# Splitting the buffers of the forms in two, and loading x for the first half's residual into the part of forms 0 and 1

## The chip, the cores and the metric

The kernel runs on one core of a Trainium2 chip. The metric is the device time of one execution in microseconds (us), inputs and outputs in HBM. A run's time is taken without the profiler; one further execution was recorded by the hardware profiler, and everything that is said below of what waits for what comes from that trace.

## The reference

A block with a linear attention and a gated feed-forward network on the same normalized input, S = 2048 tokens of D = 512 features, F = 1792, 32 heads of 16. All numbers are float32.

```
xn = layernorm(x)
q, k, v = split(xn @ wqkv)                      # 32 heads of 16
pq, pk = phi(q), phi(k)                         # phi(t) = (t + 1 if t > 0 else exp(t)) + 1e-6
kv, z = sum_s pk^T v, sum_s pk                  # per head
s = ((pq @ kv) / (pq @ z + 1e-6)) @ wo
g = silu((gelu(xn @ w_gate) * (xn @ w_up)) @ w_down)
out = x + s * g
```

## The kernel before

**Products.** float32 matmuls are done as three passes of split numbers (a high part h and a low part l: hh, then hl and lh; `sum3`, L498). Each block product is a Strassen-like scheme of seven products: for two operands cut into 2 x 2 blocks, seven combinations of blocks ("forms", numbered 0 to 6 by slot) are made of either side, and product i (1 to 7) multiplies weight form a with data form b, `PRODUCTS` (L32): 1 takes data form 0, 2 takes 1, 3 takes 2, 4 takes 6, 5 takes 3, 6 takes 4, 7 takes 5. In PSUM four running results are kept, X (products 1, 6, 7, 4, one added on the other), Y (2), Z (5, 3) and V.

**Stages.** (1) Norm, transposes, the products with wqkv, and sums for kv and z; the forms of xn are left in two large tiles of SBUF, `XT["h"]` and `XT["l"]` (L544, pool "xf", 7 slots x 4 groups of 256 tokens in transposed form). There is room for one half of the tokens, so the forms of the first four groups are written to HBM (`spill_x`, L770, in 8 DMAs of 896 KB) and come back later. (2) The FFN over the second half of the tokens (p = 1), then (3) over the first (p = 0). (4) The last stage: s = pn @ M, where M holds kv and wo together, multiplied by g and added to x.

**The last stage** works on half p = 1, then p = 0, and within each on two column blocks c = 0, 1: four blocks (1,0), (1,1), (0,0), (0,1), with the numbers 0 to 3 in the names of the PSUM tiles and the saved results (SX2 is X of block (0,0), su2_3 the second saved X of block (0,1)). In `s_forms` (L1325) the forms of pn are made: for p = 1 in the rows of `XT["h"]` and `XT["l"]`, which the FFN has done with (row r = 7a + s for form s of operand half a, L1315), for p = 0 in tiles sf0h to sf1l of pool "wp". `s_quad` (L1348) issues the products of a block and, on VectorE and GpSimd, the sums, the product with g and the residual: `x = o + r` (L1380), o being the tile "xp" with x. The results X are copied out of PSUM by ScalarE (`esaved`, L1050) into a ring of three buffers ("fe"): a copy waits until the third copy before it has been read, and TensorE may add its next product to X only after the copy.

**x for the residual** comes with `x_again` (L1408). For p = 1 it takes four tiles of pool "dp"; for p = 0 one tile "xp0" that lies in the place of `XT["h"]`, loaded by four DMAs of 512 KB:

```
whole = tile_in("xf", "h", [P, KT, HALF], F32, "xp0", 0)
```

A tile in another's place waits until every reader of the earlier tile is done.

**What sets the order.** `Plan` holds all operations with costs and dependences, TensorE's order is written out by hand (`pe_keys`; at the end L1433 to L1443), and a list scheduler with late times finds the order on the other engines, improved by a list of random changes (`STEPS`, L91, `order`, L345). VectorE, ScalarE, GpSimd and TensorE then work in exactly that order. The DMAs are all issued by SyncE, in one queue and in order; their place there follows from the program as it is emitted, and each waits in that queue for what it needs. The last blocks' products run in the order 6, 5, 7 of a block, 1 and 2 of the next, then 3 and 4.

Of the kernel before, what the change touches and what calls it, by code (L numbers as in the profile page):

```python
# [11 lines left out]
F32 = mybir.dt.float32  # L12
F32R = mybir.dt.float32r
# [4 lines left out]
P = 128  # L18
# [55 lines left out]


class Op:
    __slots__ = ("eng", "cost", "fn", "pre", "suc", "key", "name", "port", "kb", "n", "out", "use", "way", "land")


class Plan:  # L80
# [8 lines left out]
    ROUNDS = 14  # L89
    MARGIN = (0.2, 0.2, 3.0)  # L90
    STEPS = (12, 17, 30, 37, 54, 58, 64, 68, 88, 91, 95, 112, 120, 130, 135, 178, 219, 243, 254, 272, 291, 296, 307, 334, 350, 358, 391, 399, 421, 482, 518, 595, 713, 745, 884, 952, 1037, 1318, 1332, 1383, 1390, 1412, 1459, 1532, 1540, 1563, 1676, 1910, 1984, 2062, 2080, 2109, 2148, 2154, 2161, 2184, 2185, 2285, 2316, 2343, 2539, 2627, 2682, 2732, 2736, 2755, 2779, 2791, 2797, 2850, 2885, 3006, 3525, 3544, 3782, 3810, 3819, 4355, 4555, 4804, 4809, 5047, 5174, 5351)  # L91
    WAIT = 0.3
    FIXED = 4

    def __init__(self):
        self.ops = []
        self.first = 0

    def do(self, eng, cost, fn, out, *ins, more=(), key=None, name="", kb=0, kind="load"):

        op = Op()
        views = [v for v in (out, *ins) if isinstance(v, View)]
        if eng == "ACT" and any(v.psum for v in views):
            cost -= 0.04
        op.eng, op.cost, op.key, op.name = eng, cost, key, name
        op.fn = lambda: fn(out(), *[i() if isinstance(i, View) else i for i in ins])
        op.pre, op.suc = set(), []
        op.way, op.land, gap = self.MOVES[kind]
        op.kb = kb / self.RATE + gap if kb else 0.0
        op.port = eng == "POOL" or eng == "DVE" and cost > 0.25 and not any(v.psum for v in views)  # L110
        outs = set(out.res)
        for m in more:
            outs.update(m.res)
        op.out = outs
        op.use = {r for i in ins if isinstance(i, View) for r in i.res} | outs
        for i in ins:
            if isinstance(i, View):
                for r in i.res:
                    if r not in outs:
                        op.pre.update(r.writers)  # L120
                        if i.psum:
                            for d in r.readers:
                                if d.eng != eng:
                                    a, b = (op, d) if eng == "ACT" else (d, op)
                                    b.pre.add(a)
                                    a.suc.append(b)
                        r.readers.append(op)
        for r in outs:
            op.pre.update(r.writers)
            op.pre.update(r.readers)  # L130
            r.writers, r.readers = [op], []
        for v in (out, *more, *ins):
            if isinstance(v, View) and v.gen:
                assert not v.gen.over, name
                if v.gen.prev:
# [206 lines left out]
        width, size, share = rng.choice((4.0, 10.0, 25.0)), rng.choice((0.2, 0.6, 2.0)), rng.choice((0.1, 0.4, 1.0))  # L342
        return [v + rng.uniform(-size, size) if t - width < a < t + 2.0 and rng.random() < share else v for v, a in zip(late, at)]

    def order(self, pe_keys):  # L345

        late, done = self.first_order(pe_keys)
        at = self.plan_times(done)
        for seed in self.STEPS:
            late = self.nudged(late, at, seed)  # L350
            _, done = self.run(self.wide, late)
            at = self.plan_times(done)
        self.at = {self.ops[i]: t for i, t in enumerate(at)}
        self.log(max(at))
        return [self.ops[i] for i in done]
# [22 lines left out]
def kernel(  # L378
# [13 lines left out]
    nc = tc.nc  # L392
# [3 lines left out]
    KT = D // P  # L396
    NT = S // P
    NC = 512
# [4 lines left out]
    plan = Plan()  # L403
    do = plan.do
    pe_keys = []
# [51 lines left out]
    def ext(ap):  # L457
        return View((), lambda: ap)

    def dma(dst, src, kb, kind="load"):  # L460
        do("SP", 0.475, lambda o, i: nc.sync.dma_start(o, i), dst, src, kb=kb, kind=kind, name=kind)
# [76 lines left out]

    XR = {(hl, s, j): Res() for hl in "hl" for s in range(7) for j in range(4)}
    XT = {}  # L540

    def x_tiles(gen, names="hl"):
        for hl in names:
            XT[hl] = tile_in("xf", hl, [P, 7, 4, 2, P], F32R, f"X{hl}{gen}", 0)  # L544

    x_tiles(0)

    def xblock(hl, lo, hi, j):

        return XT[hl].part([XR[hl, s, j] for s in range(lo, hi)], (slice(None), slice(lo, hi), j)).map(  # L550
            lambda ap: ap.rearrange("p s k c -> p s (k c)"))

    def xslot(hl, s, j):
        return XT[hl].part([XR[hl, s, j]], (slice(None), s, j))

    def xall(hl, s):
        return XT[hl].part([XR[hl, s, j] for j in range(4)], (slice(None), s))

    def by_slot(v):
        return v.map(lambda ap: ap.rearrange("p (s k) c -> p s (k c)", k=2))  # L560
# [202 lines left out]
    def gacc(t):  # L763
        if not gps:
            gps.extend(bank(4 + c, f"gps{c}") for c in range(KT))
        for c in range(KT):
            cs = (slice(None), slice(c * P, (c + 1) * P))
            sum3(("G", t, c), gps[c], [([v[cs] for v in xn_s[t]], pk_s[t])], t == first_g, t == last_g, "gacc")

    def spill_x(n):  # L770
        for hl in "hl":
            dma(x_d[hl](n, (slice(None), slice(None), n)), xblock(hl, 0, 7, n).map(lambda ap: ap.bitcast(F32)), 896, "pieces")

    def first_products(n):
        ta = tokens[n][0]
# [533 lines left out]
    ms = [weights("W", a, f"ms{a}") for a in range(2)]  # L1309
    for a in range(2):  # L1310
        load_weights(("m", a), ms[a])
    xforms = {}
    for a in range(2):
        for s in range(7):
            r = 7 * a + s  # L1315
            for hl in "hl":
                xforms[hl, a, s] = View([XR[hl, r // 2, 2 * (r % 2) + n] for n in range(2)], XT[hl].map(
                    lambda ap, r=r: ap.rearrange("p s j k c -> p (s j k c)")[:, r * NC:(r + 1) * NC]).get, XT[hl].gen)
    BR = [12, 13, 14, 6, 7, 8, 9, 10, 11]
    HALF = 2 * NC  # L1320
    LAST = (1, 0)
# [86 lines left out]
    def x_again(p):  # L1408

        got = {}  # L1410
        if not p:
            whole = tile_in("xf", "h", [P, KT, HALF], F32, "xp0", 0)
        for k in (0, 2, 1, 3):
            got[k] = tile_in("dp", ring("br", BR), [P, HALF], F32, f"xp{p}{k}", 4) if p else whole.part(
                [Res() for _ in range(4)], (slice(None), k))
            dma(got[k], ext(xt[k * P:(k + 1) * P, p * HALF:(p + 1) * HALF]), 512, "first")
        return got

    forms, gg, xps = {}, {}, {}
    for p in (1, 0):  # L1420
        forms[p] = s_forms(p)
        if p:
# [67 lines left out]
```

## Time and profile before

| what | us |
|---|---|
| median of 3 runs | 605.6 (604.96 to 605.67) |
| profiled execution, its own time | 605.75 |
| its span, first to last instruction | 604.0 |
| TensorE busy | 593.9 |
| VectorE busy | 471.4 |
| GpSimd busy | 357.1 |
| ScalarE busy | 334.8 |
| mean granted TensorE clock | 0.993 |

The engines' names in the profile are PE (TensorE), PEld (its weight loads), DVE (VectorE), ACT (ScalarE), POOL (GpSimd) and SP or SPq (SyncE, which issues the DMAs). A row of a timeline has the start, the length, the engine, the line and the operation with its tiles, out<-in, and in brackets how long the engine had been idle and who released it. Names of tiles have their numbers left out there: SX is SX0 to SX3, Xh and Xl are the tiles of forms. One DMA of the profile is the issue; its data lands some microseconds later. In the table by stretches the columns are the stretch and its length, the busy time of each engine with its count of instructions, the granted clock (PEclk), the busy share of DMA and its GB/s. "DMA to landing" gives the least, median and longest time from issue to landing for the DMAs of one tile.

### The profile page before, as it was taken

How to read it: one execution, taken by the hardware profiler on the slowest of the kernel's cores; microseconds unless marked ns; L12 is line 12 of the kernel's file. 1: busy time of each engine (PE TensorE's matmuls, PEld its weight loads, DVE VectorE, ACT ScalarE, POOL GpSimd, SP SyncE). 2: the span in 40 equal slices, each digit the busy share in tenths (PEclk: the TensorE clock that was granted, in tenths of full speed). 3: DMA queues.
4: the chain of work that ended last, by engine and by line, in shares of the span. 5: the costliest groups of instructions: out<-in, count | busy, mean ns of one | idle time of the engine just before them, and what ended most of it. 6: DMA issues, size and time to landing. Idle time of an engine off the chain costs nothing.

```text
span 604.0 us, 8229 instructions
## 1 busy us (share of the span) xinstructions
PE 593.9 (98%) x2696; PEld 490.7 (81%) x2696; DVE 471.4 (78%) x698; ACT 334.8 (55%) x611; POOL 357.1 (59%) x300
## 2 busy tenths in 40 slices
PE   8999999999999999999999999999999999999994
PEld 7888888888888888888888888887888888887883
DVE  6999988785788878898888947556656776889995
ACT  6777777876676654564464146455134640477730
POOL 4844654525778865977598226437226752667664
PEclk9999999999999999999999999999999999999997
DMA  7459522258759637864769986888499996998347
GB/s 244 141 180 306 192 70 89 89 171 281 278 194 328 244 123 262 331 226 148 260 216 398 337 314 209 301 293 281 153 288 320 318 328 199 363 329 292 108 136 281
DMA packets 59370, 145.24 MB, mean 240 GB/s; under 512 B 5568, under 2 KB 17088, under 8 KB 59328
## 3 DMA queue, kind: packets, MB, share of 16 engines
q1 hardware_dynamic: 59328, 144.73, 68.8%
q8 instruction: 21, 0.34, 0.2%
q14 instruction: 21, 0.17, 0.1%
HBM read 82.05 MB, written 62.65 MB: 240 GB/s over the span
## 4 chain that ended last, share of the span: by engine, by line
PE 95%; DMA 2%; DVE 1%; ACT 0%; SPq 0%; issue 0%; DVEq 0%; ACTq 0%
PE FX L508 25%; PE FZ L508 13%; PE DX L508 13%; PE gps L508 7%; PE DZ L508 6%; PE FY L508 6%; PE X L508 5%; PE DY L508 3%; PE SX L508 3%; PE Z L508 3%; PE q L508 2%; PE k L508 2%; DMA xp<-in_xt 1%; PE Y L508 1%; PE ptq L1165 1%; PE pt L677 1%
## 5 line engine op out<-in xcount | busy, mean ns | idle before, releaser
L508 PE MATMUL FX<-Xh,w 128*128 128x512 f32 x448 | 152.4, 390 | 0.0
L1073 POOL TENSOR_TENSOR h<-h,g 128x512 f32<-128x512 f32 x42 | 63.1, 1508 | 69.9 <-DVE h L492 65.2
L508 PEld LDWEIGHTS FX<-Xh,w 128*128 128x128 f32 x448 | 83.7, 188 | 17.1
L492 POOL TENSOR_TENSOR h<-h,h 128x512 f32<-128x512 f32 x56 | 83.7, 1494 | 17.8 <-DVE hf5l L492 4.4
L508 PE MATMUL FX<-Xl,w 128*128 128x512 f32 x224 | 87.3, 390 | 0.0
L508 PE MATMUL FZ<-Xh,w 128*128 128x512 f32 x224 | 78.0, 390 | 0.0
L486 ACT COPY fu<-FX 128x512 f32<-128x512 f32 x56 | 32.9, 587 | 60.5 <-PE FX L508 46.4
L508 PE MATMUL gps<-pks,xns 128*128 128x512 f32 x192 | 51.2, 391 | 0.0
L508 PEld LDWEIGHTS FX<-Xl,w 128*128 128x128 f32 x224 | 42.1, 188 | 8.7
L508 PEld LDWEIGHTS FZ<-Xh,w 128*128 128x128 f32 x224 | 42.0, 188 | 8.6
L753 POOL TENSOR_TENSOR zacc<-zacc,kp 128x512 f32<-128x512 f32 x16 | 24.8, 1551 | 34.6 <-DVE kp L742 34.4
L508 PE MATMUL FZ<-Xl,w 128*128 128x512 f32 x112 | 43.7, 390 | 0.0
L492 POOL TENSOR_TENSOR u<-q,zacc 128x512 f32<-128x512 f32 x16 | 22.2, 1407 | 34.6 <-ACT g L1065 15.5
L508 PEld LDWEIGHTS gps<-pks,xns 128*128 128x128 f32 x192 | 35.9, 188 | 7.4
L1099 DVE TENSOR_TENSOR acc<-acc,DX 128x512 f32<-128x512 f32 x48 | 32.5, 684 | 9.2 <-PE DX L508 8.8
L508 PE MATMUL FY<-Xh,w 128*128 128x512 f32 x112 | 39.0, 389 | 0.0
L492 DVE TENSOR_TENSOR h<-fu,FZ 128x512 f32<-128x512 f32 x28 | 19.1, 684 | 22.7 <-PE FZ L508 15.4
L486 ACT COPY fe<-FX 128x512 f32<-128x512 f32 x28 | 16.5, 588 | 34.5 <-PE FX L508 31.1
L492 DVE TENSOR_TENSOR g<-fu,FZ 128x512 f32<-128x512 f32 x28 | 19.1, 682 | 20.3 <-PE FZ L508 13.3
L1065 ACT ACTIVATE g<-g 128x512 f32<-128x512 f32 x42 | 26.6, 633 | 13.4 <-DVE g L492 13.4
L508 PE MATMUL X<-kq,Xh 128*128 128x512 f32 x96 | 30.8, 397 | 0.0
L1099 DVE TENSOR_TENSOR acc<-acc,DZ 128x512 f32<-128x512 f32 x32 | 21.8, 682 | 10.5 <-PE DZ L508 8.9
(423 smaller groups left out, 1599.0 us busy)
## 6 DMA issues: line engine op xcount, KB each, us to landing
w_d<-w SPq DMA_DIRECT2D x36, 512.0 KB, 4.8
w<-w_d SPq DMA_DIRECT2D x36, 512.0 KB, 5.1
wd_d<-wd SPq DMA_DIRECT2D x21, 512.0 KB, 4.8
wd<-wd_d SPq DMA_DIRECT2D x21, 512.0 KB, 5.4
x<-in_first SPq DMA_DIRECT2D x16, 256.0 KB, 3.9
q_d<-qp SPq DMA_DIRECT2D x16, 256.0 KB, 2.0
q<-q_d SPq DMA_DIRECT2D x16, 256.0 KB, 5.1
pn_d<-pT SPq DMA_DIRECT2D x8, 512.0 KB, 6.1
```

The source lines that it names most:

```text
L486: do("ACT", act(n), lambda o, i: nc.scalar.copy(o, i), dst, src, name=name)
L492: do(eng, c, lambda o, p, q: getattr(e, f"tensor_{op}")(o, p, q), dst, a, b, name=name)
L508: nc.tensor.matmul(o, v[i], v[i + 1], start=start and part == 0 and i == 0, stop=stop and part == 1 and i == len(v) - 2, skip_group_check=on)
L677: nc.tensor.transpose(o[:, k, :], a[:, k * P:(k + 1) * P], b)
L753: do("POOL", pool(D), lambda o, i: nc.gpsimd.tensor_add(o, o, i), zacc, p0, name="zacc")
L1065: curved("gelu", do("ACT", curve(NC), lambda o, i: nc.scalar.activation(o, i, AF.Gelu_apprx_tanh), g, ps if e is None else g, name="gelu"))
L1073: do("POOL", pool(NC), lambda o, i: nc.gpsimd.tensor_mul(o, o, i), h, g, name="h")
L1099: do("DVE", dve(NC), lambda o, i: nc.vector.tensor_add(o, o, i), a, ps, name="acc")
L1165: nc.tensor.transpose(v[:, k, :], u[:, k * P:(k + 1) * P], idn)
```

## The change

`XT["h"]` and `XT["l"]` become two tiles each: one with slots 0 and 1 (forms 0 and 1 of xn), one with slots 2 to 6; the places in SBUF together are as large as before. In the last stage the forms of the half p = 1 are laid out so that forms 0 and 1 of both operand halves fill the first tile (`REST` has the rows of the others). `x_again(0)` takes two tiles, in the place of the first tile of h (for k = 0, 1) and of l (for k = 2, 3), so its loads wait for the products 1 and 2 of the blocks (1,0) and (1,1), and not for all products of that half. The spills, which now come from two tiles, are two DMAs each, 256 and 640 KB, 16 in all.

The planner is given the old dependences while it makes its first order and its list of changes (`held`, `steady`, `hold_rows`), then the true ones; `MORE`, a list for further changes, is empty.

```diff
@@ class Plan
+    MORE = ()
...
+    def steady(self, pe_keys):
+
+        for op, pre in self.held:
+            op.kept = set(op.pre)
+            self.free_of(op, pre)
+        late, done = self.first_order(pe_keys)
+        late, done, at = self.improved(late, done, self.plan_times(done), self.STEPS)
+        for op, _ in self.held:
+            self.free_of(op, op.kept)
...
+        _, done = self.run(self.wide, late)
+        return late, done, self.plan_times(done)
@@ the tiles of the forms
+    XCUT = ((0, 2), (2, 7))
 
     def x_tiles(gen, names="hl"):
         for hl in names:
-            XT[hl] = tile_in("xf", hl, [P, 7, 4, 2, P], F32R, f"X{hl}{gen}", 0)
+            for i, (lo, hi) in enumerate(XCUT):
+                XT[hl, i] = tile_in("xf", f"{hl}{i}", [P, hi - lo, 4, 2, P], F32R, f"X{hl}{i}{gen}", 0)
@@ the spills
+    def move_both(o, a, b):
+        nc.sync.dma_start(o[:, 0:2], a)
+        nc.sync.dma_start(o[:, 2:7], b)
+
     def spill_x(n):
         for hl in "hl":
-            dma(x_d[hl](n, (slice(None), slice(None), n)), xblock(hl, 0, 7, n).map(lambda ap: ap.bitcast(F32)), 896, "pieces")
+            a, b = [xblock(hl, *XCUT[i], n).map(lambda ap: ap.bitcast(F32)) for i in range(2)]
+            do("SP", 0.475, move_both, x_d[hl](n, (slice(None), slice(None), n)), a, b, kb=896, kind="pieces", name="pieces")
@@ the rows of the forms of the half p = 1
+    REST = (8, 9, 6, 7, 10, 11, 12, 13, 4, 5)
...
-            r = 7 * a + s
+            r = 2 * a + s if s < 2 else REST[5 * a + s - 2]
@@ x_again
-        if not p:
-            whole = tile_in("xf", "h", [P, KT, HALF], F32, "xp0", 0)
+        before = XT["h", 0].gen.ops | XT["h", 1].gen.ops
+        whole = {} if p else {hl: tile_in("xf", f"{hl}0", [P, 2, HALF], F32, f"xp0{hl}", 2) for hl in "hl"}
         for k in (0, 2, 1, 3):
-            got[k] = tile_in("dp", ring("br", BR), [P, HALF], F32, f"xp{p}{k}", 4) if p else whole.part(
-                [Res() for _ in range(4)], (slice(None), k))
+            got[k] = tile_in("dp", ring("br", BR), [P, HALF], F32, f"xp{p}{k}", 4) if p else whole["hl"[k // 2]].part(
+                [Res() for _ in range(4)], (slice(None), k % 2))
             dma(got[k], ext(xt[k * P:(k + 1) * P, p * HALF:(p + 1) * HALF]), 512, "first")
+            if not p:
+                plan.held.append((plan.ops[-1], before))
```

On TensorE, VectorE, ScalarE and GpSimd every instruction stands where it stood. On SyncE two places change. The first is the end of the queue; xp10 to xp13 are the tiles of x for p = 1, xp0 (then xp0h and xp0l) that for p = 0, pb the raw pn of which the forms of p = 0 are made, out_y the output. Before:

```order
L461 DMA pb011_5516<-pn0_d_84 128x512 x2
L461 DMA out_y<-xp12_5449 128x1024
L461 DMA out_y<-xp10_5398 128x1024
L461 DMA xp0_5649<-in_xt 128x1024 x4
L461 DMA out_y<-xp11_5308 128x1024
L461 DMA out_y<-xp13_5356 128x1024
L461 DMA out_y<-xp0_5649 128x512 x7
L461 DMA out_y<-xp0_5649 128x256 x2
```

and with the change:

```order
L490 DMA pb011_5526<-pn0_d_84 128x512 x2
L490 DMA xp0l_5567<-in_xt 128x1024
L490 DMA xp0h_5560<-in_xt 128x1024 x2
L490 DMA xp0l_5567<-in_xt 128x1024
L490 DMA out_y<-xp12_5459 128x1024
L490 DMA out_y<-xp10_5408 128x1024
L490 DMA out_y<-xp11_5318 128x1024
L490 DMA out_y<-xp13_5366 128x1024
```

The four loads of x for p = 0 have moved ahead of two stores of p = 1's output.

The second is the start, where x2, x6, x3, x7, x8 and x12 are tiles of 128 tokens of x, xh_d and xl_d the spilled forms in HBM. Before:

```order
L461 DMA x2_234<-in_first 128x512
L461 DMA x6_278<-in_first 128x512
L461 DMA x3_334<-in_first 128x512
L461 DMA x7_349<-in_first 128x512
L461 DMA xh_d_82<-Xh0_247 896x1x256 x2
L461 DMA x8_524<-in_first 128x512
L461 DMA x12_532<-in_first 128x512
L461 DMA xl_d_83<-Xl0_266 896x1x256
```

and with the change:

```order
L490 DMA x2_234<-in_first 128x512
L807 DMA xh_d_82<-Xh00_247 128x2x256
L490 DMA x6_278<-in_first 128x512
L807 DMA xl_d_83<-Xl00_266 128x2x256
L490 DMA x3_336<-in_first 128x512
L490 DMA x7_351<-in_first 128x512
L807 DMA xh_d_82<-Xh00_247 128x2x256
L807 DMA xl_d_83<-Xl00_266 128x2x256
L808 DMA xh_d_82<-Xh10_309 128x5x256 x2
L490 DMA x8_528<-in_first 128x512
L490 DMA x12_536<-in_first 128x512
L808 DMA xl_d_83<-Xl10_332 128x5x256
```

The spills of forms 0 and 1, which are made first, have moved in between the loads of x; the rest of the spills stands where the whole did.

More of the change, by code (lines that the diff above doesn't have):

```diff
@@ L76 @@
 class Op:
-    __slots__ = ("eng", "cost", "fn", "pre", "suc", "key", "name", "port", "kb", "n", "out", "use", "way", "land")
+    __slots__ = ("eng", "cost", "fn", "pre", "suc", "key", "name", "port", "kb", "n", "out", "use", "way", "land", "kept")
 class Plan:
@@ L97, in __init__ @@
         self.first = 0
+        self.held = []
     def do(self, eng, cost, fn, out, *ins, more=(), key=None, name="", kb=0, kind="load"):
@@ L343, in nudged, with improved @@
         return [v + rng.uniform(-size, size) if t - width < a < t + 2.0 and rng.random() < share else v for v, a in zip(late, at)]
[L345 to L349, printed above, removed]
+    def improved(self, late, done, at, seeds):
+        for seed in seeds:
             late = self.nudged(late, at, seed)
@@ L352, in order, with free_of @@
             at = self.plan_times(done)
+        return late, done, at
+    def free_of(self, op, pre):
+        for p in op.pre - pre:
+            p.suc.remove(op)
+        for p in pre - op.pre:
+            p.suc.append(op)
+        op.pre = pre
+    def steady(self, pe_keys):
[6 more added lines that the diff above has]
+            self.free_of(op, op.kept)
+        self.link(pe_keys, 0.0, 0.0, 0.0)
+        self.plain = self.ahead
+        self.link(pe_keys, *self.MARGIN)
+        self.wide = self.ahead
+        _, done = self.run(self.wide, late)
+        return late, done, self.plan_times(done)
+    def order(self, pe_keys):
+        _, done, at = self.improved(*self.steady(pe_keys), self.MORE)
         self.at = {self.ops[i]: t for i, t in enumerate(at)}
@@ L540 @@
     XT = {}
+    XCUT = ((0, 2), (2, 7))
     def x_tiles(gen, names="hl"):
         for hl in names:
-            XT[hl] = tile_in("xf", hl, [P, 7, 4, 2, P], F32R, f"X{hl}{gen}", 0)
+            for i, (lo, hi) in enumerate(XCUT):
+                XT[hl, i] = tile_in("xf", f"{hl}{i}", [P, hi - lo, 4, 2, P], F32R, f"X{hl}{i}{gen}", 0)
     x_tiles(0)
     def xblock(hl, lo, hi, j):
-        return XT[hl].part([XR[hl, s, j] for s in range(lo, hi)], (slice(None), slice(lo, hi), j)).map(
+        i = int(lo >= 2)
+        at = XCUT[i][0]
+        assert hi <= XCUT[i][1]
+        return XT[hl, i].part([XR[hl, s, j] for s in range(lo, hi)], (slice(None), slice(lo - at, hi - at), j)).map(
             lambda ap: ap.rearrange("p s k c -> p s (k c)"))
     def xslot(hl, s, j):
-        return XT[hl].part([XR[hl, s, j]], (slice(None), s, j))
+        i = int(s >= 2)
+        return XT[hl, i].part([XR[hl, s, j]], (slice(None), s - XCUT[i][0], j))
     def xall(hl, s):
-        return XT[hl].part([XR[hl, s, j] for j in range(4)], (slice(None), s))
+        i = int(s >= 2)
+        return XT[hl, i].part([XR[hl, s, j] for j in range(4)], (slice(None), s - XCUT[i][0]))
     def by_slot(v):
@@ L1311 @@
         load_weights(("m", a), ms[a])
-    xforms = {}
+    REST = (8, 9, 6, 7, 10, 11, 12, 13, 4, 5)
+    xforms, at_row = {}, {}
+    used = {k: set(r.writers + r.readers) for k, r in XR.items()}
     for a in range(2):
         for s in range(7):
-            r = 7 * a + s
+            r = 2 * a + s if s < 2 else REST[5 * a + s - 2]
             for hl in "hl":
-                xforms[hl, a, s] = View([XR[hl, r // 2, 2 * (r % 2) + n] for n in range(2)], XT[hl].map(
-                    lambda ap, r=r: ap.rearrange("p s j k c -> p (s j k c)")[:, r * NC:(r + 1) * NC]).get, XT[hl].gen)
+                v = XT[hl, int(s >= 2)]
+                at_row[hl, a, s] = r
+                xforms[hl, a, s] = View([XR[hl, r // 2, 2 * (r % 2) + n] for n in range(2)], v.map(
+                    lambda ap, r=r: ap.rearrange("p s j k c -> p (s j k c)")[:, (r % 4 if r < 4 else r - 4) * NC:][:, :NC]).get, v.gen)
     BR = [12, 13, 14, 6, 7, 8, 9, 10, 11]
@@ L1410, in x_again, with row_of, hold_rows @@
         got = {}
-        if not p:
-            whole = tile_in("xf", "h", [P, KT, HALF], F32, "xp0", 0)
+        before = XT["h", 0].gen.ops | XT["h", 1].gen.ops
+        whole = {} if p else {hl: tile_in("xf", f"{hl}0", [P, 2, HALF], F32, f"xp0{hl}", 2) for hl in "hl"}
         for k in (0, 2, 1, 3):
-            got[k] = tile_in("dp", ring("br", BR), [P, HALF], F32, f"xp{p}{k}", 4) if p else whole.part(
-                [Res() for _ in range(4)], (slice(None), k))
+            got[k] = tile_in("dp", ring("br", BR), [P, HALF], F32, f"xp{p}{k}", 4) if p else whole["hl"[k // 2]].part(
+                [Res() for _ in range(4)], (slice(None), k % 2))
             dma(got[k], ext(xt[k * P:(k + 1) * P, p * HALF:(p + 1) * HALF]), 512, "first")
+            if not p:
+                plan.held.append((plan.ops[-1], before))
         return got
     forms, gg, xps = {}, {}, {}
+    def row_of(hl, r):
+        return used[hl, r // 2, 2 * (r % 2)] | used[hl, r // 2, 2 * (r % 2) + 1]
+    def hold_rows(ops):
+        rows = {v.res[0]: key for key, v in xforms.items()}
+        for op in ops:
+            pre = set(op.pre)
+            for r in op.out:
+                if r in rows:
+                    hl, a, s = rows[r]
+                    pre = pre - row_of(hl, at_row[hl, a, s]) | row_of(hl, 7 * a + s)
+            if pre != op.pre:
+                plan.held.append((op, pre))
     for p in (1, 0):
+        n_ops = len(plan.ops)
         forms[p] = s_forms(p)
+        if p:
+            hold_rows(plan.ops[n_ops:])
         if p:
```

## The prediction

> **What bounds the kernel now.** The page comes first: busy time by engine, and the granted clock over the 40 slices.
>
> ```profile
> PE 593.9 (98%) x2696; PEld 490.7 (81%) x2696; DVE 471.4 (78%) x698; ACT 334.8 (55%) x611; POOL 357.1 (59%) x300
> ...
> PEclk9999999999999999999999999999999999999997
> ```
>
> TensorE is busy for 593.9 of the span's 604.0 us, so only what shortens or stops its stream counts. The clock is full in every slice but the last: whatever goes wrong does so in the last 15 us. The chain of waits for that stretch (start, length, what) shows it.
>
> ```profile
> 583.41 8.29 DMA xp<-in_xt
> ...
> 593.12 0.59 ACT su L486
> 593.75 1.76 PE SX L508 x6
> ...
> 596.23 2.94 PE SX L508 x12
> 599.20 0.44 DVE SX L492
> ```
>
> From 583.41 on the chain runs for 8.29 us through a load of x for the residual, and only then back to TensorE. Who waits for that load is in VectorE's timeline, idle time and its releaser in brackets.
>
> ```profile
> 588.26 0.68 DVE L492 TENSOR_TENSOR acc<-acc,SV 128x512 f32<-128x512 f32 x1
> 591.79 0.69 DVE L492 TENSOR_TENSOR xp<-xp,SY 128x512 f32<-128x512 f32 x1 [2.84 <-DMA xp<-in_xt]
> 592.39 0.69 DVE L492 TENSOR_TENSOR SZ<-su,SZ 128x512 f32<-128x512 f32 x1
> ```
>
> VectorE works in order. Behind the waiting residual add stands SZ<-su,SZ of block (0,0), which has its products already; ScalarE's copy su2_3 (593.12) needs the buffer that this add reads, and TensorE's product 7 of block (0,1) may overwrite X only after that copy. So a late load of x stops TensorE:
>
> ```profile
> 589.07 0.40 PE L508 MATMUL SZ<-sf1h,ms 128*128 128x512 f32 x1
> ...
> 591.35 0.39 PE L508 MATMUL SZ<-sf1h,ms 128*128 128x512 f32 x1
> 593.75 0.50 PE L508 MATMUL SX<-sf0h,ms 128*128 128x512 f32 x1 [2.02 <-ACT su L486]
> 594.09 0.39 PE L508 MATMUL SX<-sf1h,ms 128*128 128x512 f32 x1
> ...
> 595.02 0.49 PE L508 MATMUL SX<-sf1h,ms 128*128 128x512 f32 x1
> 596.23 0.58 PE L508 MATMUL SX<-sf0h,ms 128*128 128x256 f32 x1 [0.73 <-ACT su L486]
> 596.61 0.42 PE L508 MATMUL SX<-sf1h,ms 128*128 128x256 f32 x1
> ...
> 598.75 0.41 PE L508 MATMUL SX<-sf1h,ms 128*128 128x256 f32 x1
> ```
>
> Starts are 0.23 us apart up to 591.35, but 0.34 at the restart, and 0.214 at the end ((598.75 - 596.61) / 10) although those matmuls have half the columns. The table by stretches (PEclk is the third column from the end) tells why.
>
> ```profile
> 594.50:595.00 0.50, 0.50 (x3) 0.39 (x3) 0.50 (x1) 0.00 (x0) 0.50 (x1) 1.00 1.01 393
> 595.00:595.50 0.50, 0.50 (x2) 0.00 (x0) 0.47 (x2) 0.00 (x0) 0.50 (x2) 0.67 0.98 377
> 595.50:596.00 0.50, 0.00 (x1) 0.00 (x0) 0.47 (x2) 0.41 (x1) 0.50 (x1) 0.50 0.79 303
> ```
>
> The clock falls from 1.00 to 0.50 at about 595.2, 3.4 us after TensorE ran dry, and the last twelve matmuls run at half speed.
>
> **The change part by part.** First, when the loads can start. SyncE's queue before:
>
> ```profile
> 556.79 6.47 SPq L461 DMA_DIRECT2D pb<-pn_d  x6
> 573.26 8.80 SPq L461 DMA_DIRECT2D out_y<-xp  x2
> 582.17 3.07 SPq L461 DMA_DIRECT2D xp<-in_xt  x4
> ...
> SPq L461 <- POOL xp L492: 16.7, 6, 8.1
> ```
>
> The four loads stood behind two stores, the second of which waited 8.1 us for GpSimd. Now they stand ahead of both, right behind the pb loads, and wait for TensorE's last product that reads forms 0 and 1 of the first half, product 2 of block (1,1). What DMA does from 556 on, in 40 slices of 0.475 us:
>
> ```profile
> 565.46 0.39 PE L508 MATMUL SY<-Xh,ms 128*128 128x512 f32 x1
> ...
> GB/s 138 69 259 319 233 220 233 229 263 336 306 323 332 164 35 78 203 185 332 289 17 17 0 0 0 0 0 0 0 0 0 0 0 0 0 34 0 0 379 414
> ...
> DMA to landing us min/median/max: 1.9/4.9/9.2
> ...
> 588.61 1.29 POOL L492 TENSOR_TENSOR xp<-xp,acc 128x512 f32<-128x512 f32 x1
> ```
>
> That product ends at 565.46 + 0.39 = 565.85, and from 566.4 to 572.6 nothing is moved at all: the loads fall into a hole. With the old spacing (3.07 us for four) the last is issued by 569, and with the worst landing time of this tile (9.2 us) it is there at 578.2, ten microseconds before its first reader at 588.61. The stores behind them keep their times, since the first left at 573.26.
>
> Then what the missing wait is worth, step by step. VectorE's successive starts lie 0.60 us apart (591.79 to 592.39), so the residual add starts at 588.26 + 0.60 = 588.86. SZ<-su,SZ would be next at 589.46; its products end at 589.07 + 0.40 = 589.47, and with the 0.04 us of a hop (599.16 to 599.20 at the end) it starts at 589.51, ends at 590.20. ScalarE copies from 590.24 to 590.83, and product 7 may start at 590.87. TensorE is busy until then: its last matmul before it starts at 591.35, the next turn is 591.58. The copy is 0.7 us early, TensorE waits for nothing, and the start moves from 593.75 to 591.58: 2.17 us. The restart's 0.11 us (0.34 - 0.23) and the last matmul's 0.10 (0.49 - 0.39, half of it at the lower clock) go too: product 7 ends at 591.58 + 5 x 0.227 + 0.39 = 593.10 and not 595.51, **2.41 us** earlier. What comes late next is the second copy of X, a true dependence that stays: 0.73 us of idle before the half products.
>
> Next the clock. If TensorE isn't idle for 2 us, does the clock hold? The trace has one other gap of that order, at the start:
>
> ```profile
> 9.34 0.50 PE L508 MATMUL k<-kq,Xl 128*128 128x512 f32 x1 [0.94 <-DVE Xl L492]
> ...
> 9.00:10.00 1.00, 0.66 (x3) 0.58 (x4) 0.74 (x2) 0.94 (x2) 0.39 (x1) 1.00 1.03 391
> ```
>
> There 0.94 us of idle left the clock at 1.00, and here 0.73 remain: I take it that the clock holds. The price of a 256-column matmul at full clock is in no row. Its bounds: 0.214 us (the half clock's pitch, if the clock doesn't matter) and that of the transposes, 128 columns with a weight load each:
>
> ```profile
> 528.74 0.87 PE ptq L1165 x8
> ```
>
> 0.87 / 8 = 0.109. I take 0.115, near the lower end, since half of the 512-column pitch of 0.227 is 0.114. Twelve then take 0.115 + 0.11 (restart) + 10 x 0.115 + 0.28 (the 0.39 of a 512-column one less 0.11) = 1.66 us where they took 2.93: **1.27 us**, between 0 and 1.34. VectorE's last four operations and the last store follow TensorE's end as before.
>
> The Trainium skill, page "TensorE: Matmul & The Clock Gate", section "Part 1: The HAM clock gate", has the clock halved only after at least one idle window of about 3.4 us. The trace does not agree to the letter: 2.02 us of idle were enough here, though the fall came one such length after the stall began. By that rule the fall would not be this stall's doing, and the sum would stop at 2.41; that is the first rival.
>
> The other rows of the forms: the forms of the first half go to rows in another order, so their writers wait for other readers of the second FFN pass.
>
> ```profile
> 535.55 1.36 PE FZ L508 x6
> ...
> 545.69 0.60 ACT L486 CAST Xh<-pb 128x512 fp32r<-128x512 f32 x1
> ```
>
> The last such product ends at 536.91, the first form is written at 545.69: nothing is gained or lost. Four engines keep their order.
>
> The spills: 8 of 896 KB become 16 of 256 and 640 KB, the same bytes, and SyncE's order at the start changes: half spills stand among the loads of the x tiles.
>
> ```profile
> 12.08 0.41 DVE L492 TENSOR_TENSOR Xl<-pt,Xh 128x256 fp32r<-128x256 f32 x1
> 27.38 0.69 DVE L646 BATCH_NORM_STATS2 st<-x 128x6 f32<-128x512 f32 x1
> ...
> 14.02 1.21 SPq L461 DMA_DIRECT2D x<-in_first  x2
> ...
> DMA to landing us min/median/max: 2.4/3.9/7.6
> ...
> 20.00:60.00 40.00, 40.00 (x186) 33.09 (x185) 37.15 (x64) 28.61 (x50) 21.32 (x18) 1.00 0.67 223
> ```
>
> The worst placed one (the low part of the first pair) waits for VectorE until 12.49, and the loads behind it were issued at 14.02 for reasons of their own. The last of them, issued by 15.2 and there by 22.8 with the longest landing time of an x tile (7.6), is read at 27.38: 4.5 us of cover, and TensorE is full from 20 to 60. I cost the spills at nothing; without that cover, up to 256 KB at the 391 GB/s of 9 to 10 us, 0.7 us, for each of the first two half spills, 1.3 us together; shorter pieces could also free the forms earlier, but no engine waits for them, so no gain.
>
> **The sum.** 2.41 + 1.27 = 3.68 us off the profiled execution's 605.75: 602.07. That execution lay 0.15 above the median of the runs (605.6), so I forecast **602.0**.
>
> **The rivals.**
> *The clock falls all the same* (for it: one fall in the whole trace, close before the end, so its cause is inferred from one case; against: it came 3.4 us after the stall, and a gap of 0.94 us left it alone). Then only the 2.41 us go: 605.75 - 2.41 - 0.15 = 603.2. Chance 0.19.
> *Another wait takes the place.* The copy has 0.7 us in hand. GpSimd's adds into the same tile then come earlier and run beside the two VectorE operations ahead of the copy. If these took 1.7 us each and not 0.69 (2 us more), product 7 would start at 592.9, 0.9 us earlier than before, with a stall of 1.3 us: 604.7. Against it: the same kinds of operation, each with an operand in PSUM, took 0.68 to 0.69 above. Chance 0.06.
> *The change doesn't do what it says*: the loads are held until the last product that reads any form of that half. The queue order speaks against a later time than this:
>
> ```profile
> 577.25 0.39 PE L508 MATMUL SZ<-Xh,ms 128*128 128x512 f32 x1
> ```
>
> Issued from 577.7, 4.5 us earlier than 582.17, the one that lands at 591.70 lands at 587.2, still ahead of 588.86: the same 602.0. It would take loads behind the second store, issued after 581.7, to leave 605.6: chance 0.02.
> *Slower: the x tiles starve at the start.* A half spill stands in SyncE's queue ahead of x3 and x7; if it left late, the norms of those tiles, the transposes and every product behind them would follow. It decides once those loads land over 4.5 us later than with the worst landing time so far; each further microsecond costs one, and it must also eat the 3.7 us won, so the loads would have to be 8.2 us late and more for a time above 605.6; at 10 us late 607.4. Nothing in the rows holds the half spill beyond 12.49. Chance 0.05.
>
> **How the numbers follow.** The forecast has 0.68: 601.2 (the shortest 256-column pitch, and the 0.64 us by which the lowest run, 604.96, lay under the median) to 602.8. Taking in the first rival, with half a microsecond for the uncovered spills, the range is 601.2 to 603.7. A difference counts from 0.2%, 1.2 us, about what a measurement of this kernel can tell from no change. Forecast, first rival and a little of the second lie more than that below 605.6: faster 0.89; the rest of the second, and the third: same 0.06; slower 0.05.
>
> **What would show it.** Right: the four loads issued near 566, no bracket with xp on VectorE's residual add near 588.9, product 7 following product 3 without idle, a clock of 1.00 to the end and 256-column matmuls near 0.115 us apart. Wrong: a clock of 0.50 in the last stretch (first rival), an idle TensorE of over 0.3 us ahead of product 7 with another releaser than the load (second), any idle of TensorE between 12 and 60 us that before didn't have (last).

## The result, and the profile after

The changed kernel took 603.0 us (median of 5 runs, 602.39 to 603.48), the kernel before beside it 605.67 (604.96 to 607.7): a ratio of 0.995, with a 95% interval of 0.9933 to 0.9968. Three more sets of the changed kernel, with nothing altered, are among the experiments. The profiled execution took 603.29 us, with a span of 601.6; before, 605.75 and 604.0. So 605.75 - 603.29 = 2.46 us of the forecast 3.68 are there in the two traces.

The page of the changed kernel, busy time and granted clock, has the same work on TensorE in 1.1 us less, and no slice at the end with a lower clock.

```profile
PE 592.8 (99%) x2696; PEld 489.2 (81%) x2696; DVE 471.0 (78%) x698; ACT 334.7 (56%) x611; POOL 356.3 (59%) x300
...
PEclk9999999999999999999999999999999999999999
```

SyncE's queue (start, length, issues): the loads leave from 566.10 on, ahead of the stores, which start at 573.68 where they started at 573.26.

```profile
566.10 0.33 SPq L490 DMA_DIRECT2D xp0l<-in_xt  x1
566.53 0.90 SPq L490 DMA_DIRECT2D xp0h<-in_xt  x2
567.48 0.48 SPq L490 DMA_DIRECT2D xp0l<-in_xt  x1
573.68 10.65 SPq L490 DMA_DIRECT2D out_y<-xp  x4
...
597.50 1.31 SPq L490 DMA_DIRECT2D out_y<-xp0l  x3
```

All engines at the end of the changed kernel, in order of time. The residual add xp0h<-xp0h,SY at 589.46 waits for nothing (2.84 us before). Product 7 starts at 592.38, one spacing (0.23) behind the last matmul of product 3: no idle time. The 256-column matmuls are (596.04 - 594.85) / 10 = 0.119 us apart. The wait of 0.73 us for the second copy is still there.

```profile
589.46 0.68 DVE L521 TENSOR_TENSOR xp0h<-xp0h,SY 128x512 f32<-128x512 f32 x1
...
590.31 0.70 DVE L521 TENSOR_TENSOR SZ<-su,SZ 128x512 f32<-128x512 f32 x1 [0.17 <-PE SZ L537]
...
591.04 0.59 ACT L515 COPY su<-SX 128x512 f32<-128x512 f32 x1 [1.95 <-DVE SZ L521]
...
592.15 0.39 PE L537 MATMUL SZ<-sf1h,ms 128*128 128x512 f32 x1
592.38 0.39 PE L537 MATMUL SX<-sf0h,ms 128*128 128x512 f32 x1
...
594.63 0.38 PE L537 MATMUL SX<-sf0h,ms 128*128 128x256 f32 x1 [0.73 <-ACT su L515]
594.85 0.28 PE L537 MATMUL SX<-sf1h,ms 128*128 128x256 f32 x1
...
596.04 0.28 PE L537 MATMUL SX<-sf1h,ms 128*128 128x256 f32 x1
596.21 1.26 POOL L521 TENSOR_TENSOR xp0l<-xp0l,acc 128x512 f32<-128x512 f32 x1 [1.86 <-DVE acc L521]
596.35 0.43 DVE L521 TENSOR_TENSOR SX<-acc,SX 128x256 f32<-128x256 f32 x1 [0.23 <-PE SX L537]
...
597.73 0.42 DVE L521 TENSOR_TENSOR xp0l<-xp0l,SX 128x256 f32<-128x256 f32 x1
```

From VectorE's last add (597.73 + 0.42 = 598.15) to the end of the span are 3.45 us; before it was 604.0 - 601.0 = 3.0. GpSimd's last add, which ended with TensorE before, now ends at 597.47, 1.15 us after TensorE (596.32). Its store stands in SyncE's queue ahead of VectorE's last two; the three leave together from 597.50 on.

### The profile page after: what moved, and what is told of

The parts are those of the page before. It is cut to its first block, busy times and chain, and to the rows that moved or that the text cites. A ratio compares the mean times of both kernels' runs of the same rounds, so it can differ in the third digit from the quotient of the medians.

```text
span 601.6 us, 8255 instructions
## 1 busy us (share of the span) xinstructions
PE 592.8 (99%) x2696; PEld 489.2 (81%) x2696; DVE 471.0 (78%) x698; ACT 334.7 (56%) x611; POOL 356.3 (59%) x300
## 4 chain that ended last, share of the span: by engine, by line
PE 97%; DVE 2%; DMA 1%; ACT 0%; SPq 0%; issue 0%; ACTq 0%
PE FX L537 25%; PE FZ L537 13%; PE DX L537 13%; PE gps L537 7%; PE DZ L537 6%; PE FY L537 6%; PE X L537 5%; PE SX L537 4%; PE DY L537 3%; PE Z L537 3%; PE q L537 2%; PE k L537 2%; PE SZ L537 2%; PE Y L537 1%; PE ptq L1206 1%; PE pt L713 1%
```

## The experiments

Theory: x comes early enough, so the stall of 2 us goes (2.41 us); and without the stall the clock doesn't fall (1.27 us). Rivals: the split and the rows themselves bring or cost something; the clock falls in any case; or the stall matters only because of the clock. "Kept the clock" below means a mean granted clock of 0.995 or more in an execution, "fell" one of 0.994 or less: the line is drawn between the two groups, and a fall behind TensorE's last product (in the first repeat's profile at 598.5, mean 0.998) changes nothing. Ratios are to the kernel before on the same chip.

**The changed kernel again,** in three sets.

> The changed kernel once more, unaltered, to see which differences between two executions are scatter. Forecast theory (a late load held VectorE, VectorE held ScalarE's copy, the copy held TensorE for 2.0 us, and that idle halved the clock for the last twelve matmuls): 603.0 us, clock 1.00 to the end, no idle ahead of product 7 of block (0,1). Of the 0.80 us by which that product started later than the forecast's 591.58, 0.44 had gathered by 560 and 0.36 at 577 to 580; if these are scatter, another execution has them at other places or not at all, if they belong to the change, they stand at the same places again.

> The changed kernel unaltered, beside the one above on the same chip. Theory: median 2.2 to 2.7 us below the kernel before (ratio 0.995 to 0.9965), no execution with a mean granted clock of 0.994 or less, while before has some 3 in 10 of these. Rival (the gain is the clock's alone): the median is that of the executions of before that kept the clock, and differs from them by less than 0.5 us.

> The changed kernel unaltered, for the two above on the same chip: 603.0 to 603.2, the span ends 4.1 us after GpSimd's last add.

Measured: 603.18 us (8 runs, ratio 0.9963, 0.995 to 0.9976), 603.12 (6 runs, 0.9964, 0.9952 to 0.9975) and 603.15 (6 runs, 0.9946, 0.9928 to 0.9964). All the executions of these two kernels whose clock was listed, put together, mean time and standard deviation:

```
kernel before, clock fell   27 of 83   606.86  (0.80)
kernel before, clock kept   56 of 83   605.47  (0.69)
kernel changed, clock fell   0 of 25
kernel changed, clock kept  25 of 25   603.24  (0.63)
```

The profiled execution of before was one of the minority. In the other two thirds the clock kept at full, so there was no clock term to win. No trace of such an execution is on record: that it had the stall of 2 us is inferred, from the same program and from the 2.2 us that it loses against the changed kernel. Against these two thirds the change wins 605.47 - 603.24 = 2.23 us, against the others 606.86 - 603.24 = 3.62.

**The whole change, but with the load late:** x in one tile again, in the place of the second tile of h.

```diff
-        whole = {} if p else {hl: tile_in("xf", f"{hl}0", [P, 2, HALF], F32, f"xp0{hl}", 2) for hl in "hl"}
+        whole = None if p else tile_in("xf", "h1", [P, KT, HALF], F32, "xp0", 0)
...
```

> Everything of the change but the early load: x for the half p = 0 is one tile again, in the place of the second tile of h (forms 2 to 6), so that its four loads stand behind the two stores as they did before. Forecast theory: 605.6 us (605.0 to 606.2), the loads issued near 582, VectorE idle for 2 to 3 us ahead of the residual add, TensorE idle 2 us, clock 0.50 at the end. Rival (the finer spills or the other rows of the forms brought the gain): 603.0 us. A cost of the 16 spills would show as a time above 605.7.

Measured: 605.67 us (11 runs), ratio 0.9997 (0.9983 to 1.0011). Its SyncE, VectorE and TensorE show before's picture once more.

```profile
574.13 8.83 SPq L490 DMA_DIRECT2D out_y<-xp  x2
583.07 2.93 SPq L490 DMA_DIRECT2D xp<-in_xt  x4
```

```profile
592.69 0.69 DVE L521 TENSOR_TENSOR xp<-xp,SY 128x512 f32<-128x512 f32 x1 [2.85 <-DMA xp<-in_xt]
...
594.65 0.50 PE L537 MATMUL SX<-sf0h,ms 128*128 128x512 f32 x1 [2.05 <-ACT su L515]
```

The split, the 16 spills and the new rows are worth nothing to within 1 us; to within that, the early load is the whole gain. The clock fell in 3 of 11.

**The kernel before with its stall filled:** eight small matmuls of ones (16 instructions in the trace), into a bank of PSUM that is free by then, ahead of product 7.

```diff
...
+        if o.key == ("S", 0, 1, 7) and not filled:
+            filled = True
+            warm(spare[3]()[:, 0:P], ones(), 8)
```

> The kernel before, with eight matmuls of a constant (128 columns, 0.22 us each) put into TensorE's queue ahead of product 7 of block (0,1), into a PSUM tile that nobody reads any more: the stall on the load stays, but TensorE is busy in it. Forecast theory (the idle halves the clock): product 7 starts as late as before, the clock stays at 1.00, the 256-column matmuls come 0.12 us apart, and the end is 0.8 to 1.3 us earlier: 604.4 to 604.9 us. Rival (the clock falls near the end for another reason, as the rule of a whole idle window of 3.4 us would have it): 605.7 us, clock 0.50, 0.214 us apart.

Measured: 605.7 us (11 runs), ratio 0.9998 (0.9987 to 1.0008). The wait for x is as before and product 7 starts late, but the clock never fell while TensorE worked, and the half products run at full speed.

```profile
591.09 1.95 PE L530 MATMUL SY<-ones 128*128 128x128 f32 x16
591.27 0.69 DVE L492 TENSOR_TENSOR xp<-xp,SY 128x512 f32<-128x512 f32 x1 [2.81 <-DMA xp<-in_xt]
...
593.23 0.50 PE L508 MATMUL SX<-sf0h,ms 128*128 128x512 f32 x1 [0.20 <-ACT su L486]
```

So idle TensorE is what makes the clock fall: none of 11, where the kernel beside it had 9 of 31. Yet the median is no better, 0.8 us above what the theory said, since it is made by executions that keep the clock without help: the eleven have a mean of 605.52, those of before that kept the clock 605.47.

**The changed kernel with the stall put back,** and with it made shorter and longer: 8, 6 and 12 copies on ScalarE ahead of su2_3, of a tile onto itself.

```diff
+        if o.name == "su2_3":
+            for _ in range(8):
+                nc.scalar.copy(zacc(), zacc())
```

> The changed kernel with eight copies of a tile that is no longer needed on ScalarE ahead of the copy su2_3, some 4.8 us: the loads are early as in the change, but the copy comes late again, so that TensorE is idle for about 2.0 us ahead of product 7. Forecast theory (only the stall and the clock matter, not the load itself): the 2.0 us of idle and a clock of 0.50 at the end come back, 605.2 to 606.0 us. Rival (the burst of loads at the end slowed the kernel by itself, through its traffic or the stores behind it): idle of 2.0 us but less than the whole time back, 604.0 to 604.9 us, with the clock at 1.00.

> The changed kernel with six copies on ScalarE ahead of su2_3 (eight left 2.17 us of idle TensorE; one copy is 0.59 us, so about 1.0 us here). Theory (the stall itself costs its length in every execution, the clock falls only after a longer one): product 7 starts about 1.0 us late, the time is 604.0 to 604.9, and no execution has a mean granted clock of 0.994 or less. Rival (the clock falls in some executions with a chance in proportion to the idle time, 9 of 31 at 2.0 us): about 14%, one or two executions of eleven at 0.994 or less, and those about 1.3 us above the others.

> The changed kernel with twelve copies on ScalarE ahead of su2_3, about 4.5 us of idle TensorE ahead of product 7. Without a fall of the clock: 606.1 (the eight copies in executions that kept the clock) + 4 x 0.59 = 608.5. Theory (the fall comes some 3.4 us after TensorE ran dry, and the longer the idle time the more often): the clock has fallen before TensorE restarts in all or nearly all executions, product 7 and the half products run at half speed, some 1.3 us each, and the median is 610 to 611.2, mean granted clock at most 0.992. Rival (whether the clock falls depends on the execution alone, about 3 in 10 whatever the length): median 608.5, a third of the executions higher.

Idle ahead of product 7 is from each profile, the rest from all executions:

```
copies   idle us   median us   ratio (95%)               clock fell
6        1.05      604.64      0.9983 (0.9966 to 1.0001)    0 of 12
8        2.17      606.53      1.0012 (1.0 to 1.0025)       4 of 11
12       4.96      610.09      1.0067 (1.0051 to 1.0083)    5 of 6
```

The first matmul of product 7 with 6, 8 and 12 copies, from three traces:

```profile
592.68 0.50 PE L537 MATMUL SX<-sf0h,ms 128*128 128x512 f32 x1 [1.05 <-ACT su L515]
...
594.70 0.50 PE L537 MATMUL SX<-sf0h,ms 128*128 128x512 f32 x1 [2.17 <-ACT su L515]
...
596.69 0.80 PE L537 MATMUL SX<-sf0h,ms 128*128 128x512 f32 x1 [4.96 <-ACT su L515]
```

With 2.17 us of idle the gain is gone, and that without the clock too: the seven executions that kept it have a mean of 606.12, and the median is 0.5 us above the expected range. With 1.05 the clock holds, as the theory had it, though at one or two of twelve the rival's miss is weak evidence. The long stall decides: the rival's 3 in 10 whatever the length is wrong. Even in the sixth execution, the profiled one, the clock fell, and came back. Its table by stretches (PEclk third from the end), with five rows of 0.25 us:

```profile
596.00:596.25 0.25, 0.00 (x0) 0.00 (x0) 0.00 (x0) 0.25 (x2) 0.00 (x0) 1.00 0.00 0
596.25:596.50 0.25, 0.00 (x0) 0.00 (x0) 0.00 (x0) 0.25 (x1) 0.00 (x0) 0.53 0.00 0
...
599.25:599.50 0.25, 0.25 (x1) 0.00 (x0) 0.00 (x0) 0.00 (x0) 0.00 (x0) 0.50 0.00 0
599.50:599.75 0.25, 0.12 (x1) 0.00 (x0) 0.00 (x0) 0.04 (x1) 0.00 (x0) 0.65 0.21 82
...
606.50:606.75 0.25, 0.00 (x0) 0.00 (x0) 0.00 (x0) 0.00 (x0) 0.00 (x0) 0.51 0.00 0
```

A stretch with a share f of its time at full reads 0.5 + f/2: the fall is at 596.27, the return at 599.67, 3.41 us apart, though TensorE was idle from 591.73 on and busy again from 596.69. Behind TensorE's last product (which ended at 602.05) the clock falls once more, at 606.50, two times 3.41 us after the return. None of the three comes at a fixed distance from the start or the end of an idle time: they lie on a beat of 3.41 us that runs by itself. Falls of other traces, in the first two rows with the late load and the stall put back, at 595.81 and 595.60:

```profile
595.50:596.00 0.50, 0.50 (x4) 0.34 (x2) 0.47 (x2) 0.00 (x0) 0.50 (x1) 0.81 1.04 402
...
595.50:596.00 0.50, 0.50 (x3) 0.39 (x2) 0.50 (x1) 0.00 (x0) 0.00 (x0) 0.60 0.74 275
...
598.50:599.00 0.50, 0.00 (x0) 0.00 (x0) 0.09 (x1) 0.00 (x0) 0.00 (x0) 0.70 0.63 238
...
602.50:602.70 0.20, 0.00 (x0) 0.00 (x0) 0.00 (x0) 0.00 (x0) 0.00 (x0) 0.53 0.00 0
```

In these two, and before (595.17), the 3.41 us up to the fall hold the idle time whole (to 0.02 us in the last): 592.60 to 594.65, 592.53 to 594.70 and 591.74 to 593.75. The other two rows are falls behind the last product, which cost nothing but bound the rule. In the short stall (6 copies) the clock fell at 598.70, with 1.95 us of idle in the stretch. With the filled stall it fell at 602.51 and not one beat earlier, at 599.10, where the stretch had 1.80 us of idle (TensorE ended at 597.30). So the clock seems to fall at the end of such a stretch when between 1.80 and 1.95 us of it, or more, are idle; this is a reading of a few traces. An idle time of 2.0 us falls whole into one stretch with a chance of (3.41 - 2.0) / 3.41 = 41%; 27 of 83, 3 of 11 and 4 of 11 were seen (33, 27 and 36%), none at 1.05 us. The shares lie below that estimate; how long the idle time was in the executions without a trace isn't known. The Trainium skill, "TensorE: Matmul & The Clock Gate", section "Part 1: The HAM clock gate", has a free-running window of 3413 ns: the 3.41 us here agree. Its condition for a fall, one idle window, doesn't: 2.0 us were enough.

**The other idle time taken away:** su2_3 in a buffer of its own, product 7 of block (0,1) ahead of product 3, so that no copy is waited for; one residual add goes from VectorE to GpSimd.

```diff
...
+                    kept.append(pools["up"].tile([P, D], F32, name=name, tag=f"up{FC[0]}", bufs=1))
...
+                if (n, dh, th) == (3, 0, 1):
+                    plan.ops[-2].fn = lambda: nc.vector.tensor_mul(v(), v(), to())
+                    plan.ops[-1].fn = lambda: nc.gpsimd.tensor_add(x(), x(), v())
...
+    seq[-31:] = [end[i] for i in turns]
```

> The changed kernel with the other idle time at the end taken away: su2_3 has a buffer of its own and is copied as soon as product 6 is through, product 7 of block (0,1) runs ahead of product 3, so that product 3 covers the copy su3_3; one residual add is moved from VectorE to GpSimd. Theory (at the end the kernel hangs on this chain alone): no idle of TensorE over 0.3 us after 580, TensorE ends 0.7 us or more earlier, VectorE's last add about 0.7 us earlier, time 602.2 to 602.8. Rival (VectorE has its last operations to do one after the other, whenever X comes): TensorE ends earlier, VectorE's last add stays within 0.2 us of where it was, time 602.9 to 603.2.

Measured: 604.12 us (9 runs), ratio 0.9972 (0.9959 to 0.9984). TensorE ends at 594.65, 1.7 us earlier than in the changed kernel's trace, and nothing comes of it: the rival's case, and 0.9 us worse than it said. Of VectorE and GpSimd:

```profile
592.47 1.29 POOL L521 TENSOR_TENSOR xp0l<-xp0l,acc 128x512 f32<-128x512 f32 x1
592.57 1.75 DVE L521 TENSOR_TENSOR SV<-su,sz 128x512 f32<-128x512 f32 x1 [0.93 <-ACT su L515]
...
597.66 0.42 DVE L521 TENSOR_TENSOR xp0l<-xp0l,SX 128x256 f32<-128x256 f32 x1
597.74 0.33 SPq L490 DMA_DIRECT2D out_y<-xp0h  x1
```

The sum SV<-su,sz, whose two inputs are both in SBUF, took 1.75 us beside GpSimd's add; VectorE ends at 598.08, 0.07 earlier than in the changed kernel. With the sum of Z put ahead of it:

```diff
-    turns = (0, 7, 9, 2, 4, 5, 6, 10, 13, 12, 15, 1, 3, 16, 20, 24, 29, 8, 11, 14, 17, 19, 21, 22, 23, 25, 27, 18, 26, 28, 30)
+    turns = (0, 7, 9, 2, 4, 5, 6, 10, 13, 12, 15, 1, 3, 8, 16, 20, 24, 29, 11, 14, 17, 19, 21, 22, 23, 25, 27, 18, 26, 28, 30)
```

> As the kernel without idle, but on VectorE the sum SZ<-su,SZ of block (0,1) ahead of SV<-su,sz, which took 1.75 us there, beside GpSimd's add, where it took 0.69 with GpSimd idle. Theory (VectorE's own chain now sets the end, and 1.06 us of it were that meeting): SV takes about 0.7 us again, VectorE's last add ends about 0.6 us earlier than in the kernel without idle, and the time is 0.5 us or so below that of the changed kernel in the same runs. Rival (the end of the kernel is not set by VectorE's last add but by the stores behind it, three of which now come close together): the last add is earlier, but the time is that of the changed kernel or up to 1 us above it.

Measured: 604.0 us (11 runs), ratio 0.9973 (0.9963 to 0.9983), beside 603.12 for the changed kernel in the same runs. SV takes 0.70 us again, VectorE ends at 597.31, and the span still at 601.7: the rival's case again.

```profile
593.59 0.70 DVE L521 TENSOR_TENSOR SV<-su,sz 128x512 f32<-128x512 f32 x1
...
596.31 1.27 POOL L1436 TENSOR_TENSOR xp0h<-xp0h,acc 128x512 f32<-128x512 f32 x1
...
596.89 0.42 DVE L521 TENSOR_TENSOR xp0l<-xp0l,SX 128x256 f32<-128x256 f32 x1
597.60 0.33 SPq L490 DMA_DIRECT2D out_y<-xp0h  x1
598.02 0.89 SPq L490 DMA_DIRECT2D out_y<-xp0l  x2
```

What ends the span here seems to be GpSimd's last add, at 597.58, and the stores that queue behind it. The span ends 4.04 to 4.13 us after GpSimd's last add in all four profiles of the changed kernel, in the filled stall (4.08), in the short and the long one (4.09, 4.11) and in these two (4.09, 4.12). Where the half products ran at half clock (before, late load, stall put back) it ends 2.98 to 3.0 after VectorE's.

**The stores apart:** in the changed kernel the store behind GpSimd's last add issued by ScalarE; and the same for GpSimd's last two in the version above.

```diff
+                    if (n, dh, th) in ((3, 1, 1),):
+                        plan.ops[-1].fn = lambda x=x, k=k, lo=lo, w=w: nc.scalar.dma_start(out[k * P:(k + 1) * P, lo:lo + w], x())
```

> The changed kernel with one DMA moved: the store behind GpSimd's last add, which stands in SyncE's queue ahead of VectorE's last two stores, is issued by ScalarE. Theory (in the changed kernel the span ends 4.09 to 4.13 us after GpSimd's last add, by that store and the two behind it): SyncE issues VectorE's stores as they come, the span ends 3.0 us after VectorE's last add as in the kernel before, 0.3 to 0.5 us earlier against the other marks, time 602.4 to 602.9. Rival (the 4.1 us are the landing of GpSimd's own store and the end of the program): no change, 603.0 to 603.2.

> The kernel without idle and with the two sums turned round, and GpSimd's last two stores issued by ScalarE. VectorE's last add ended at 597.31 there and GpSimd's at 597.58, and the span at 601.7. Theory: the span ends 3.0 us after VectorE's last add or about as much after GpSimd's, near 600.5, the time is about 1 us below the version with these stores in SyncE's queue (604.0): 602.8 to 603.1. Rival (the last adds do not set the end): 603.7 to 604.2 again.

Measured: 603.39 us (6 runs, ratio 0.9952, 0.9933 to 0.9971) and 603.53 (10 runs, 0.9958, 0.9943 to 0.9974), beside 603.15 for the changed kernel on that chip. Both lie 0.4 us or more above what the theory said. The trace of the first has part of the effect: its span of 600.7 ends 3.84 us after GpSimd's add, and 3.16 after VectorE's, where 3.0 were expected. In the second the span (601.4) ends 3.50 us after GpSimd's last add and 3.76 after VectorE's, 0.9 later than expected.

```profile
595.60 1.26 POOL L521 TENSOR_TENSOR xp0l<-xp0l,acc 128x512 f32<-128x512 f32 x1 [1.79 <-DVE acc L521]
...
596.66 1.25 SPq L490 DMA_DIRECT2D out_y<-xp0l  x2
...
596.89 0.37 ACTq L1429 DMA_DIRECT2D out_y<-xp0l  x1
597.12 0.42 DVE L521 TENSOR_TENSOR xp0l<-xp0l,SX 128x256 f32<-128x256 f32 x1
```

0.3 us lie below what these runs can tell. None of the four versions beats the changed kernel; why the last two without idle time have medians 0.9 and 0.4 us above it on the same chip, when their profiled spans (601.7, 601.4) are no longer than its own there (602.0, 602.3), stays open. These spans are of one execution each: that of 601.7 was the fastest of its eleven, that of 602.3 the slowest of its six.

## Why the prediction was right, and where it was not

**The loads** did as forecast, issued near 566 into the hole of the DMAs. **The stall** went as forecast: no wait of the residual add, and product 7 on product 3 without idle. 2.41 us were forecast; the means of executions that kept the clock give 2.23, give or take 0.3 by their deviations, and with the late load all of it is lost again.

**The clock** held in every execution, and the 256-column matmuls took 0.119 us and not 0.115. So the first rival was wrong: the idle time was the cause, as the filled stall shows. The term itself is right too, 606.86 - 605.47 = 1.39 where 1.27 were forecast. What was wrong is how often it is there: one trace was taken for the kernel, and a third of the executions for all of them. "It came 3.4 us after the stall" was a coincidence of where that beat lay; with the late load it came 3.2 us after the idle time began, with the long stall 4.5.

**The step that failed** is the last of the sum: "that execution lay 0.15 above the median of the runs (605.6), so I forecast 602.0." The execution was of the kind with the fall, which has a mean of 606.86, and lay 1.1 us below that mean; it came to stand next to the median by scatter. 3.68 off its own kind's mean is 603.18, where the changed kernel is (603.24). For the median, which two executions in three without a fall make, the sum had to be 605.47 - 2.41 = 603.06; measured 603.0 to 603.18. So the median lies 1.0 us above 602.0 and outside the 601.2 to 602.8 of the forecast itself. It lies inside the wider range, up to 603.7, only because that took in the first rival, whose 603.2 came nearly true by luck: it left the clock term out because the clock would fall after the change too, where in fact the median before had no such term.

**In the two traces** the same shows as scatter and as one term left out. Product 7 started at 592.38 and not at 591.58: 0.80 us, of which 0.44 had gathered by 560, before the loads, and 0.36 came at 577 to 580, where a difference sf0l on VectorE took 1.82 us beside GpSimd; in the next profile of the same kernel (602.41) neither delay is there and product 7 starts at 591.52. The wider spacing is 0.04. "VectorE's last four operations and the last store follow TensorE's end as before" failed by 0.45: at full clock GpSimd's last add ends after TensorE, and its store holds up the two behind it. 602.07 + 0.80 + 0.04 + 0.45 = 603.36, against 603.29. For the median this term is probably nothing, since the kernel before, where it keeps the clock, should end by GpSimd's add as well: with the stall filled it does (4.08).

**The rows of the forms and the spills** cost and brought nothing to within 1 us, as forecast. **Another wait in the place**: none came. Its price of 1.7 us for a VectorE operation beside GpSimd is real (1.82, 1.75 us), but not for operations with an operand in PSUM, which stood there: SZ<-su,SZ took 0.70 beside GpSimd's add at 590.31. **The x tiles** did not starve.

## What to carry to other kernels

A load that stands in an in-order queue behind a waiting store can stop an engine three steps on; follow the wait from the load to the reader, and to what stands behind the reader. Before an event near the end of one trace is priced, look at the mean clock of the other executions: an event with a chance of a third is worth a third of its price on average, and nothing on the median. When the last engine gets faster, look at which of the others' last stores is next in the queue, since the remaining idle time of TensorE was worth nothing in the versions tried here.

## What the hardware showed that was not expected

- The granted clock fell and came back 3.41 us apart, on a beat that did not start with the idle time. About 2 us of idle in one such stretch were enough in every traced fall (1.95 the least); a stretch with 1.80 us had none, and a stall of 1.05 us never made the clock fall ahead of the last products (0 of 12).
- At half clock 256-column float32 matmuls are 0.214 us apart, at full 0.119.
- A VectorE operation on inputs that are all in SBUF takes 1.75 or 1.82 us beside GpSimd where it takes 0.69 or 0.70 otherwise; with one input in PSUM it took 0.70 beside GpSimd too.
- Where three stores (256, 128 and 128 KB) are issued one behind the other, the span ends 4.04 to 4.13 us after the add that makes the first of them ready; with the first on another queue it was 3.84, in one trace.
